# A fused decode block on one core: 768 instead of 512 columns of each partition's last wq row are loaded onto other partitions

## The chip, the core and the metric

The kernel runs on one core of a Trainium2 chip. All times are microseconds of device time. Three runs of the kernel before are shown: 137.84, 137.85 and 137.92 us, median 137.85 us. The profile is of one separate execution. A core has five engines with instruction streams of their own (TensorE, here PE, with its weight loads as PEld; VectorE, DVE; ScalarE, ACT; GpSimd, POOL; SyncE, SP), and sixteen DMA engines that move data between HBM and the on-chip memory SBUF, whose 128 partitions are the rows of every tile.

## The reference

One token for each of four sequences goes through an attention block over a window of 2048 cached keys, and then through a gated MLP. Cut to what is computed:

```python
h = x + A(layernorm(x))             # x: 4 x 1 x 1024
#   q = xn @ wq                     # wq 1024 x 4096: 32 heads of 128
#   k, v = last 2048 rows of each cache, 4 kv heads of 128
#   A = softmax(q k^T / sqrt(128)) v @ wo
h2 = h + B(layernorm(h))
#   B = (silu(hn @ w1) * (hn @ w3)) @ w2     # F = 3584
```

All inputs and the output are bf16. Weights and cache windows together make 55.6 MB that have to be read once.

## The kernel before

The kernel is a stream of large loads, all issued on SP's queue, and the arithmetic that follows it. The loads go into `ring`, one SBUF tile of 160 KiB per partition, used in a circle by hand: the `plan` list says which part of which tensor goes to which offset (`KIB = 512` elements is one KiB), and `load_next()` issues the next entry of the plan at the places in the program where its old contents have been read. The order of the stream is wq rows 0 to 3 of each partition, the side loads, wq rows 4 to 7 (the tail), the k cache (four loads), the v cache (four), wo, w1, w3, and w2 in four pieces. Semaphores made by the framework hold a load back until the readers of its place are done.

wq is laid out so that partition p holds rows 8p to 8p+7 of the 1024 x 4096 matrix (`wq_v`, `KC = 8`). For each of the eight rows the loop at line 263 issues eight matmuls of 512 columns into `q_ps`, with the matching column of the normalised x as the stationary operand (`xnT`, four columns). `JG = 4` groups of columns lie in four stripes of 32 partitions of `q_ps`.

The exception is the end of the last row. The last `CE = 512` columns of row 8p+7 are left out of the tail load (`load_tail`, L126). They come through `load_side` (L120) onto other partitions: `SETS` has triples (first row group r0, ne, ns), and a set takes ne x 4 x ns rows and puts them on ne x 4 partitions, ns pieces on each. The first set has 80 rows on 20 partitions, the second 48 rows on 12. For them the same values of x are gathered in a different order: copies into `xs` (L206), transposes into `ts_ps` (L211), copies into `xsT` (L218), and, after the fourth row's matmuls, eight small matmuls (L273) that add into the same part of `q_ps`. The row loop then skips these columns.

The side tiles of the kernel before come from the pool `ktpool`, which has four buffers that later hold transposed keys. The first seven entries of the plan are issued at the start; the eighth (v, second half) is issued at `kc == RQ - 1`, in program order before the side matmuls.

After q follow the key transposes (L319), the scores (L304), the softmax, the value matmuls (L382), wo (L411), the second layernorm, w1 and w3 (L459), silu and the product, and w2 (L492). The last w2 rows are loaded in pieces of 17, 7, 3 and 1 rows of each partition (4352, 1792, 768 and 256 KB), so that little work follows the last byte; two 512-column accumulators, `ya_ps` and `yb_ps`, take rows 17 to 27, and the residual is added into them by a matmul with the identity (L507).

Of the kernel before, what the change touches and what calls it, by code (L numbers as in the profile page):

```python
# [10 lines left out]
P = 128  # L11
# [3 lines left out]
BF16 = mybir.dt.bfloat16  # L15
# [4 lines left out]
def kernel(  # L20
# [13 lines left out]
    nc = tc.nc  # L34

    B, _, D = A_x.shape
# [5 lines left out]
    KC = D // P  # L42
# [15 lines left out]
    ktpool = ctx.enter_context(tc.tile_pool(name="ktpool", bufs=4))  # L58
    wide = ctx.enter_context(tc.tile_pool(name="wide", bufs=2))
    const = ctx.enter_context(tc.tile_pool(name="const", bufs=1))  # L60
    act = ctx.enter_context(tc.tile_pool(name="act", bufs=1))
# [3 lines left out]
    JG = 4  # L65
    QD = P // JG
    RS = QD // B
    CQ = Hq * Dh // JG
# [20 lines left out]
    ring = stream.tile([P, RING], BF16)  # L89
# [19 lines left out]
    N_Q, N_F = Hq * Dh, F  # L109


    CE = 512
    SETS = [(0, 5, 4), (80, 3, 4)]

    def load_side(r0, ne, ns):

        t = ktpool.tile([P, JG * QD * 16], BF16, tag="kT")
        rows = A_wq[r0 * KC : (r0 + ne * 4 * ns) * KC, N_Q - CE : N_Q]
        rows = rows.rearrange("(t i k) n -> k i t n", i=ne, k=KC)[KC - 1]
        nc.sync.dma_start(out=t[: ne * 4, : ns * CE], in_=rows)  # L120
        return [t[: ne * 4, k * CE : (k + 1) * CE] for k in range(ns)]

    def load_tail(at, src, n, r0, m):

        t = ring[:, at : at + m * n]
        nc.sync.dma_start(out=t[:, : m * n - CE], in_=src[:, r0 * n : (r0 + m) * n - CE])  # L126
        return [t[:, k * n : (k + 1) * n] for k in range(m)]
    KIB = 512
    plan = [
        ("wq", load_rows, (0, wq_v, N_Q, 0, 4)),  # L130
        ("side", load_side, SETS[0]),
        ("side", load_side, SETS[1]),
        ("wq", load_tail, (32 * KIB, wq_v, N_Q, 4, 4)),
        ("k", load_kv, (64 * KIB, A_k_cache, 0)),
        ("k", load_kv, (96 * KIB, A_k_cache, 2)),
# [10 lines left out]
    loaded = {}  # L146
    cursor = [0]

    def load_next(n=1):
        for _ in range(n):  # L150
            if cursor[0] < len(plan):
                kind, f, args = plan[cursor[0]]
                loaded.setdefault(kind, []).extend(f(*args))
                cursor[0] += 1
# [13 lines left out]
    for c in range(2):  # L168
        nc.sync.dma_start(
            out=x_q[c * 2 * QD : (c + 1) * 2 * QD : RS, :],  # L170
            in_=x_flat.rearrange("b (j c) -> j b c", j=JG)[2 * c : 2 * c + 2],
# [7 lines left out]
    for c in range(2):  # L179
# [8 lines left out]
        out=xn[:], in0=x_sb[:], scalar1=mv[:, 0:1], scalar2=rstd[:, 0:1],  # L188
# [9 lines left out]

    NS = sum(ns for _, _, ns in SETS)
    ts_ps = psA.tile([P, NS, B], BF16, tag="kt1")  # L200
    xs = wide.tile([B, NS, 20], BF16, tag="w4k")
    sl = []
    for r0, ne, ns in SETS:
        v = xn[:, r0 * KC : (r0 + ne * 4 * ns) * KC]
        v = v.rearrange("b (s l i k) -> b k l i s", s=4, l=ns, i=ne)
        nc.vector.tensor_copy(  # L206
            out=xs[:, len(sl) : len(sl) + ns, : ne * 4].rearrange("b l (i s) -> b l i s", s=4),
            in_=v[:, KC - 1, :, :, :],
        )
        for l in range(ns):  # L210
            nc.tensor.transpose(  # L211
                out=ts_ps[: ne * 4, len(sl), :], in_=xs[:, len(sl), : ne * 4], identity=ident[:B, :B]
            )
            sl.append(ne * 4)
    xsT = act.tile([20, NS, B], BF16)
    k0 = 0
    for _, ne, ns in SETS:
        nc.vector.tensor_copy(out=xsT[: ne * 4, k0 : k0 + ns, :], in_=ts_ps[: ne * 4, k0 : k0 + ns, :])  # L218
# [3 lines left out]
    q_ps = psA.tile([P, CQ], FP32, tag="scores")  # L222
# [9 lines left out]
        out=perm[:].rearrange("p (h dq) -> p h dq", dq=JG),  # L232
        in_=ident[:].rearrange("p (dq h) -> p h dq", dq=JG),
# [12 lines left out]
    for j in range(2, JG):  # L246
        nc.vector.tensor_tensor(
            out=same[:, 0, :], in0=same[:, 0, :], in1=ident[:, j * QD : (j + 1) * QD], op=ALU.add
# [6 lines left out]
    for kc in range(KC):  # L255
        wq_t = loaded["wq"][kc]
        for hf in range(CQ // 512):
            for g in range(JG):
                c0 = g * CQ + hf * 512
                n = min(512, N_Q - CE - c0) if kc == KC - 1 else 512  # L260
                if n <= 0:
                    continue
                nc.tensor.matmul(  # L263
                    q_ps[QD * g : QD * g + B, hf * 512 : hf * 512 + n],
                    lhsT=xnT[:, kc, :],
                    rhs=wq_t[:, c0 : c0 + n],
                    start=(kc == 0),
                    stop=(kc == KC - 1 or (kc == KC - 2 and c0 + 512 == N_Q)),
                )
        if kc == RQ - 1:  # L270
            load_next()
            for k, np_ in enumerate(sl):
                nc.tensor.matmul(  # L273
                    q_ps[QD * (JG - 1) : QD * (JG - 1) + B, CQ - CE : CQ],
                    lhsT=xsT[:np_, k, :],
                    rhs=loaded["side"][k],
                    start=False,
                    stop=False,
                )
    q_sb = act.tile([P, CQ], BF16)  # L280
    nc.vector.tensor_single_scalar(out=q_sb[:, :512], in_=q_ps[:, :512], scalar=qscale, op=ALU.mult)
    nc.scalar.mul(out=q_sb[:, 512:], in_=q_ps[:, 512:], mul=qscale)
# [1 line left out]
    for r in range(REP):  # L284
        nc.tensor.transpose(out=qt_ps[:, r, :], in_=q_sb[:, r * Dh : (r + 1) * Dh], identity=ident[:])
    nc.vector.tensor_copy(
        out=qz[:, :, : Hkv * QD].rearrange("p b (g z) -> p b g z", g=Hkv)[:, :, :, :REP],
        in_=qt_ps[:].rearrange("p r (g x) -> p x g r", g=Hkv)[:, :B, :, :],
# [24 lines left out]
    for u, (b, n) in enumerate(units):  # L313
        k_v = loaded["k"][b]
        kT = ktpool.tile([P, NJ, P], BF16, tag="kT")
        for t in range(NJ // TB):
            kt_ps = psA.tile([P, TB, P], BF16, tag=f"kt{nt % 4}")
            for jj in range(TB):
                nc.tensor.transpose(  # L319
                    out=kt_ps[:, jj, :], in_=k_v[:, n * NJ + t * TB + jj, :], identity=ident[:]  # L320
# [21 lines left out]
        out=Pm[:], in_=scores_ps[:], func=ACT.Exp, bias=nmax[:], scale=1.0, accum_out=rsum[:]  # L342
# [6 lines left out]
    for c in range(NSB):  # L349
# [4 lines left out]
        for g in range(Hkv):  # L354
            if g % 2 == 0:
                nc.vector.tensor_scalar(  # L356
                    out=z[:, :, g, :], in0=pt_ps[:], scalar1=mask[:, g : g + 1], scalar2=None, op0=ALU.mult
# [10 lines left out]
        out=Dm[:], in0=ident[:].rearrange("p (g b r) -> p b g r", g=Hkv, b=B),  # L368
# [11 lines left out]
    for b in range(B):  # L380
        for j in range(JK):
            nc.tensor.matmul(  # L382
                OT_ps[:, b, :],
                lhsT=loaded["v"][b][:, j, :],
                rhs=PTz[j // NJ][:, (j % NJ) * B + b, :, :],
                start=(j == 0),
                stop=(j == JK - 1),
# [21 lines left out]
    for i in range(IO):  # L409
        for j in range(JG):  # L410
            nc.tensor.matmul(  # L411
                y_ps[QD * j : QD * (j + 1), :],
                lhsT=o4[:, i, :, :].rearrange("p b s -> p (b s)"),
                rhs=loaded["wo"][i][:, j * CG : (j + 1) * CG],
                start=(i == 0),
                stop=(i == IO - 1),
# [27 lines left out]
        out=hn[:], in0=h1[:], scalar1=tot[:, 0:1], scalar2=rstd2[:, 0:1],  # L444
# [5 lines left out]
        out=hnT[:].rearrange("p k x -> p (k x)"), in_=hn[:].rearrange("q (c k) -> q k c", k=KC)  # L450
# [3 lines left out]
    def gate_up(kind, out_ps):  # L454
# [27 lines left out]
        out=hgT[:].rearrange("p i x -> p (i x)"),  # L482
        in_=hg[:].rearrange("q s c -> q (s c)").rearrange("q (c i) -> q i c", i=IF),
# [18 lines left out]
    for i in range(R1, IF):  # L502
        for c, t in enumerate((ya_ps, yb_ps)):
            down(i, HC, c * HC, t, start=(i == R1), stop=(i == IF - 1), skip_group_check=True)
        if i == R2 - 1:
            for c, t in enumerate((ya_ps, yb_ps)):
                nc.tensor.matmul(  # L507
                    t[:, :HC], lhsT=ident_f[:], rhs=h2[:, c * HC : (c + 1) * HC],
                    start=False, stop=False, skip_group_check=True,
# [36 lines left out]
```

## Time and profile before

| what | value |
|---|---|
| median of three runs | 137.85 us (137.84 to 137.92) |
| span of the profiled execution, first to last instruction | 136.0 us |
| what lies around the span, median less span | 1.85 us |
| PE busy, ACT busy, DVE busy | 72.3, 31.0, 43.9 us |
| DMA queue q1 (SP): share of sixteen engines' span | 95.6% |
| moved, mean rate | 55.75 MB, 410 GB/s |
| share of the DMA engines between 30 and 60 us | 1.01 |

The profile gives the span of its execution and no other time for it; the time around the span is therefore the difference to the median run. A share of the DMA engines near 1 means that all sixteen are at work. A share is counted by the transfers that start in a stretch, so that it can come out a little above 1. Next to the instructions, the trace keeps every DMA transfer with its queue, start, duration and size. A load of 128 partitions is one transfer for each partition, eight on each of sixteen engines. Each engine ends its share of a load with a transfer of 4 bytes, which counts up a semaphore.

### The profile page before, as it was taken

How to read it: one execution, taken by the hardware profiler on the slowest of the kernel's cores; microseconds unless marked ns; L12 is line 12 of the kernel's file. 1: busy time of each engine (PE TensorE's matmuls, PEld its weight loads, DVE VectorE, ACT ScalarE, POOL GpSimd, SP SyncE). 2: the span in 40 equal slices, each digit the busy share in tenths (PEclk: the TensorE clock that was granted, in tenths of full speed). 3: DMA queues.
4: the chain of work that ended last, by engine and by line, in shares of the span. 5: the costliest groups of instructions: out<-in, count | busy, mean ns of one | idle time of the engine just before them, and what ended most of it. 6: DMA issues, size and time to landing. Idle time of an engine off the chain costs nothing.

```text
span 136.0 us, 2436 instructions
## 1 busy us (share of the span) xinstructions
PE 72.3 (53%) x1096; PEld 46.1 (34%) x1096; DVE 43.9 (32%) x79; ACT 31.0 (23%) x36; POOL 1.7 (1%) x8
## 2 busy tenths in 40 slices
PE   0004920979898989810525916791097000970981
PEld 0002300268374756500014905570043000430870
DVE  5055000043344444470994001206200596026010
ACT  3000000015555555609294300000001400000000
POOL 5000000000000000000000000000000000000000
PEclk9999975557999999985555555568556855568568
DMA  5999999999999999999989999989989899999970
GB/s 155 464 463 406 412 420 414 429 424 439 424 439 424 424 443 426 410 552 453 463 347 463 463 410 405 477 354 494 439 371 494 371 472 401 399 420 407 424 298 5
DMA packets 2650, 55.75 MB, mean 410 GB/s; under 512 B 296, under 2 KB 464, under 8 KB 720
## 3 DMA queue, kind: packets, MB, share of 16 engines
q1 hardware_dynamic: 2604, 55.58, 95.6%
q8 instruction: 8, 0.13, 0.3%
q10 hardware_dynamic: 36, 0.02, 0.0%
q14 instruction: 2, 0.02, 0.0%
HBM read 55.59 MB, written 0.01 MB: 409 GB/s over the span
## 4 chain that ended last, share of the span: by engine, by line
DMA 54%; PE 25%; ACT 11%; DVE 5%; SPq 2%; issue 1%; ACTq 0%
DMA ring<-in_B_w_dram 38%; DMA ring<-in_A_wq_dram 15%; PE kt_ps L319 11%; ACT kT L325 5%; PE scores_ps L304 5%; ACT z L360 3%; PE q_ps L263 3%; DVE rmax L336 2%; ACT Pm L341 2%; PE OT_ps L382 2%; DVE pT L350 1%; SPq L120 1%; PE g_ps L459 1%; DVE z L356 1%; ACT L341 1%
## 5 line engine op out<-in xcount | busy, mean ns | idle before, releaser
L325 ACT COPY kT<-kt_ps 128x1024 bf16<-128x1024 bf16 x16 | 15.9, 1013 | 13.4 <-PE kt_ps L319 13.4
L319 PE MATMUL kt_ps<-ident,ring 128*128 128x128 bf16 x256 | 18.0, 232 | 0.0
L319 PEld LDWEIGHTS <-ring 128*128 128x128 bf16 x256 | 16.0, 105 | 4.9 <-issue 4.9
L323 DVE COPY kT<-kt_ps 128x1024 bf16<-128x1024 bf16 x16 | 11.1, 692 | 16.5 <-PE kt_ps L319 16.5
L459 PEld LDWEIGHTS <-hnT 128*32 128x32 bf16 x128 | 5.5, 143 | 21.8 <-issue 19.2
L382 PE MATMUL OT_ps<-z,ring 128*128 128x32 bf16 x256 | 7.5, 188 | 8.5 <-ACT z L360 5.0
L459 PE MATMUL u_ps<-ring,hnT 128*32 128x448 bf16 x64 | 6.0, 563 | 11.0 <-DMA ring<-in_B_w_dram 11.0
L304 PE MATMUL scores_ps<-kT,qz 128*32 128x512 bf16 x64 | 9.9, 609 | 2.9 <-ACT kT L325 2.9
L263 PE MATMUL q_ps<-ring,xnT 128*4 128x512 bf16 x63 | 6.7, 595 | 7.8 <-DMA ring<-in_A_wq_dram 7.8
L382 PEld LDWEIGHTS <-ring 128*128 128x128 bf16 x256 | 7.4, 104 | 9.2 <-issue 9.2
L459 PE MATMUL g_ps<-ring,hnT 128*32 128x448 bf16 x64 | 5.9, 558 | 4.9 <-DMA ring<-in_B_w_dram 4.9
L492 PEld LDWEIGHTS <-hgT 128*32 128x32 bf16 x156 | 4.9, 134 | 6.2 <-issue 5.7
L411 PE MATMUL y_ps<-ring,o 128*32 128x256 bf16 x128 | 5.9, 371 | 0.8 <-DVE o L398 0.8
L514 ACT CAST res<-yb_ps 128x128 bf16<-128x128 f32 x1 | 0.3, 266 | 26.1 <-PE yb_ps L492 26.1
L492 PE MATMUL y_ps<-ring,hgT 128*32 128x256 bf16 x68 | 3.8, 419 | 4.4 <-DMA ring<-in_B_w_dram 4.4
L360 ACT ACTIVATE z<-pt_ps,mask 128x512 bf16<-128x512 f32 x8 | 5.3, 687 | 3.5 <-DVE z L356 3.5
L352 PE MATMUL pt_ps<-pT,perm 128*128 128x512 bf16 x4 | 2.4, 607 | 6.8 <-DVE pT L350 6.8
L263 PEld LDWEIGHTS <-xnT 128*4 128x4 bf16 x63 | 2.0, 115 | 11.7 <-issue 11.6
L194 PE MATMUL tp_ps<-ident,xn 4*128 4x4 bf16 x8 | 0.7, 200 | 10.0 <-DVE xn L187 10.0
L356 DVE TENSOR_SCALAR z<-pt_ps,mask 128x512 bf16<-128x512 f32 x8 | 5.5, 741 | 1.2 <-ACT z L360 0.8
L473 DVE RECIPROCAL eg<-eg 128x896 f32<-128x896 f32 x1 | 5.8, 5753 | 0.0
L411 PEld LDWEIGHTS <-o 128*32 128x32 bf16 x128 | 4.4, 131 | 3.1 <-DVE o L398 1.9
(85 smaller groups left out, 50.1 us busy)
## 6 DMA issues: line engine op xcount, KB each, us to landing
ring<-in_B_w_dram SPq DMA_DIRECT2D x2, 7168.0 KB, 22.5
ring<-in_A_k_cache_dram SPq DMA_DIRECT2D x4, 2048.0 KB, 27.6
ring<-in_A_v_cache_dram SPq DMA_DIRECT2D x4, 2048.0 KB, 29.2
ring<-in_B_w_dram SPq DMA_DIRECT2D x1, 4352.0 KB
ring<-in_A_wq_dram SPq DMA_DIRECT2D x1, 4096.0 KB, 12.2
ring<-in_A_wq_dram SPq DMA_DIRECT2D x1, 3968.0 KB
ring<-in_B_w_dram SPq DMA_DIRECT2D x1, 1792.0 KB
ring<-in_B_w_dram SPq DMA_DIRECT2D x1, 768.0 KB
```

The source lines that it names most:

```text
L263: nc.tensor.matmul(q_ps[QD * g : QD * g + B, hf * 512 : hf * 512 + n], lhsT=xnT[:, kc, :], rhs=wq_t[:, c0 : c0 + n], start=(kc == 0), stop ...
L304: nc.tensor.matmul(scores_ps[QD * g : QD * (g + 1), n * 512 : (n + 1) * 512], lhsT=qz_v[:, z0 : z0 + QD], rhs=kT_v[:, g, :, :], start=(b = ...
L319: nc.tensor.transpose(out=kt_ps[:, jj, :], in_=k_v[:, n * NJ + t * TB + jj, :], identity=ident[:])
L323: nc.vector.tensor_copy(out=kT[:, t * TB : (t + 1) * TB, :], in_=kt_ps[:])
L325: nc.scalar.copy(out=kT[:, t * TB : (t + 1) * TB, :], in_=kt_ps[:])
L356: nc.vector.tensor_scalar(out=z[:, :, g, :], in0=pt_ps[:], scalar1=mask[:, g : g + 1], scalar2=None, op0=ALU.mult)
L360: nc.scalar.mul(out=z[:, :, g, :], in_=pt_ps[:], mul=mask[:, g : g + 1])
L382: nc.tensor.matmul(OT_ps[:, b, :], lhsT=loaded["v"][b][:, j, :], rhs=PTz[j // NJ][:, (j % NJ) * B + b, :, :], start=(j == 0), stop=(j == J ...
L411: nc.tensor.matmul(y_ps[QD * j : QD * (j + 1), :], lhsT=o4[:, i, :, :].rearrange("p b s -> p (b s)"), rhs=loaded["wo"][i][:, j * CG : (j + ...
L459: nc.tensor.matmul(out_ps[QD * j : QD * (j + 1), hf, :HF], lhsT=hnT[:, k, :], rhs=loaded[kind][k][:, c0 : c0 + HF], start=(k == 0), stop=( ...
L473: nc.vector.reciprocal(out=eg[:], in_=eg[:])
L492: nc.tensor.matmul(out_ps[QD * j : QD * (j + 1), :n], lhsT=hgT[:, i, :], rhs=loaded["w2"][i][:, j * CG + c0 : j * CG + c0 + n], **kw,)
```

## The change

`CE` goes from 512 to 768 and the 128 rows are dealt out differently: 96 rows on 32 partitions, 24 rows on 12, 8 rows on 4. The side tiles move from `ktpool` into `ring` at 128, 136 and 140 KiB, the place of the first half of v. So that half of v can be issued only when the side matmuls have read them, and both halves of v are now issued together, after the side matmuls in program order; the two small loads of `x_q` thereby come ahead of v on SP's queue. Since 768 columns span two PSUM banks, each side piece takes two matmuls, of 256 and 512 columns.

```diff
-    CE = 512
-    SETS = [(0, 5, 4), (80, 3, 4)]
-    def load_side(r0, ne, ns):
-        t = ktpool.tile([P, JG * QD * 16], BF16, tag="kT")
+    CE = 768
+    SETS = [(0, 8, 3), (96, 3, 2), (120, 1, 2)]
+    SIDE = [(max(CQ - CE, c), min(c + 512, CQ)) for c in range(0, CQ, 512) if c + 512 > CQ - CE]
+    def load_side(at, r0, ne, ns):
+        t = ring[: ne * 4, at : at + ns * CE]
         rows = A_wq[r0 * KC : (r0 + ne * 4 * ns) * KC, N_Q - CE : N_Q]
         rows = rows.rearrange("(t i k) n -> k i t n", i=ne, k=KC)[KC - 1]
-        nc.sync.dma_start(out=t[: ne * 4, : ns * CE], in_=rows)
-        return [t[: ne * 4, k * CE : (k + 1) * CE] for k in range(ns)]
+        nc.sync.dma_start(out=t, in_=rows)
+        return [t[:, k * CE : (k + 1) * CE] for k in range(ns)]
...
-        ("side", load_side, SETS[0]),
-        ("side", load_side, SETS[1]),
+        ("side", load_side, (128 * KIB, *SETS[0])),
+        ("side", load_side, (136 * KIB, *SETS[1])),
+        ("side", load_side, (140 * KIB, *SETS[2])),
...
-    xs = wide.tile([B, NS, 20], BF16, tag="w4k")
+    xs = wide.tile([B, NS, QD], BF16, tag="w4k")
...
-    xsT = act.tile([20, NS, B], BF16)
+    xsT = act.tile([QD, NS, B], BF16)
...
-                    stop=(kc == KC - 1 or (kc == KC - 2 and c0 + 512 == N_Q)),
+                    stop=(kc == KC - 1 or (kc == KC - 2 and c0 >= N_Q - CE)),
...
         if kc == RQ - 1:
-            load_next()
             for k, np_ in enumerate(sl):
-                nc.tensor.matmul(
-                    q_ps[QD * (JG - 1) : QD * (JG - 1) + B, CQ - CE : CQ],
-                    lhsT=xsT[:np_, k, :],
-                    rhs=loaded["side"][k],
-                    start=False,
-                    stop=False,
-                )
+                for c0, c1 in SIDE:
+                    nc.tensor.matmul(
+                        q_ps[QD * (JG - 1) : QD * (JG - 1) + B, c0:c1],
+                        lhsT=xsT[:np_, k, :],
+                        rhs=loaded["side"][k][:, c0 - (CQ - CE) : c1 - (CQ - CE)],
+                        start=False,
+                        stop=False,
+                    )
+            load_next(2)
```

## The prediction

> **What bounds the kernel now.** I read the page first, then the chain that ended last, then the work by windows of time, and last the single transfers in the trace.
>
> The page:
>
> ```profile
> span 136.0 us, 2436 instructions
> PE 72.3 (53%) x1096; PEld 46.1 (34%) x1096; DVE 43.9 (32%) x79; ACT 31.0 (23%) x36; POOL 1.7 (1%) x8
> DMA  5999999999999999999989999989989899999970
> q1 hardware_dynamic: 2604, 55.58, 95.6%
> q8 instruction: 8, 0.13, 0.3%
> ```
>
> No instruction engine is over 53% busy; the sixteen DMA engines are full from the second slice to the end. Queue q8 carries eight loads of PE's own program, which matter below. The chain of waits between 96 and 136 us (start, us, what):
>
> ```profile
> 76.27 22.49 DMA ring<-in_B_w_dram
> 98.80 1.68 PE g_ps L459 x14
> 100.48 29.74 DMA ring<-in_B_w_dram
> 130.22 0.04 issue
> 130.27 0.30 PE ya_ps L492 x3
> ...
> 131.82 0.42 PE ya_ps L507 x2
> 132.24 0.22 PE yb_ps L507 x2
> 132.46 0.17 PE ya_ps L492 x4
> ...
> 133.08 0.27 ACT res L514
> ```
>
> The end is released by w2 rows landing (130.22), then 2.8 us of PE. Windows (us, busy by engine, then granted PE clock, DMA share, GB/s):
>
> ```profile
> 30.00:60.00 30.00, 25.64 (x314) 17.27 (x311) 12.45 (x17) 15.90 (x16) 0.00 (x0) 0.96 1.01 430
> ...
> 130.60:131.10 0.50, 0.50 (x30) 0.50 (x25) 0.00 (x0) 0.00 (x0) 0.00 (x0) 0.50 0.93 369
> 131.30:131.80 0.50, 0.50 (x28) 0.40 (x17) 0.00 (x0) 0.00 (x0) 0.00 (x0) 0.75 0.65 250
> 131.80:132.20 0.40, 0.40 (x8) 0.40 (x4) 0.00 (x0) 0.00 (x0) 0.00 (x0) 1.00 0.60 230
> ```
>
> In mid stream all sixteen work (1.01); in the last microsecond only 0.60 to 0.65: some DMA engines are done early. So the end is set by the slowest DMA engine, and the even share is the quantity to follow. The trace's transfer records give it. On one engine the next transfer's record begins some 3 ns before the last one's ends, so records string into sixteen chains, and the 4-byte transfers show when each chain finishes a load. Finish times of two loads, us, sorted:
>
> ```
> wq tail: 21.39 21.50 21.53 21.64 21.64 21.66 21.70 21.73 21.76 21.85 21.95 | 22.15 22.34 | 22.97 22.99 23.30
> last w2: 130.60 130.84 131.02 131.24 | 131.88 132.00 and ten more, from 132.14 to 132.38
> ```
>
> At the tail there are eleven engines without side pieces (call them C), two with the 16 pieces of the first side load (B), and the same three with 16 of each (A): the three-way load lies on engines that also had the five-way one, so shares fill from the same end. A piece of 1024 bytes comes every 42.4 ns, 32 of them make 1.36 us; that is A's lag. By the end twelve are late. Each of the eight q8 loads (16 KB, starting at 32.0, 43.7, 54.6, 79.6, 86.1, 92.6, 105.2, 130.6) sets one chain back by 1.42 us, and the chains say that these are eight different engines, all of them in C. A program load on q14 at 60.6 cost one of B 0.85 us. So the twelve late are A, one of B (the one that also carries the four-way `x_sb` load; it ends near 132.26) and eight of C; early are the other B (131.24) and the three of C without a program load (130.60, 130.84, 131.02). The side loads before had put A level with the eight.
>
> **The change part by part.**
>
> *Tail load, 512 bytes less on 128 partitions.* Start-to-start on a full engine is 607.5 ns for 16384 bytes and 1284 for 34816, 37.6 ns per KB: 18.8 ns per transfer, eight on each engine, so every engine gains 0.150 us.
>
> *Side pieces.* 1536 bytes does not occur. Neighbours: 23.6 ns at 512 bytes, 42.4 at 1024, 79.9 at 2048; these lie on one line (18.8 per 512), which gives 61.2 ns. Bounds are 42.4 and 79.9; I take the line. The first load has 8 x 12 pieces: A, B and three of C get 12 (0.734 us). The second has 3 x 8: A (0.490). The third, 8 rows on 4 partitions, is four-way: A and one B, two each (0.122); by the same end-filling as `x_sb` I take the B with the 0.85 us.
>
> Net against before, tail included (A also has one more 4-byte transfer, 0.006):
>
> - A: 1.346 - 1.357 + 0.006 - 0.150 = -0.155
> - the B near 132.26: 0.857 - 0.678 + 0.006 - 0.150 = +0.035, so 132.30
> - the other B: 0.734 - 0.678 - 0.150 = -0.094
> - three of C: 0.734 + 0.006 - 0.150 = +0.59
> - the other eight of C: -0.150
>
> If the three of C are those without a program load they end at 131.2 to 131.6, still early. A's last goes 132.38 to 132.23, the eight's last 132.34 to 132.19, and the late B at 132.30 is then last. The stream ends 0.08 us earlier. Row prices at their bounds move A by 22 x 0.0188 = 0.41 either way: at the lower bound B still leads at -0.23 (132.03, with the eight at 132.19 last: -0.19), at the upper A ends at 132.64, +0.26.
>
> One rule of the Trainium skill speaks against the change: "DMA: Bandwidth & Descriptors", section "Latency and other measured facts", says copies whose row pitch is a large power of two run slower, at 512 KiB pitch 207 GB/s against 214. Successive pieces of one engine are 8 rows of 64 KiB apart in the new first load (320 KiB before). By it the 0.73 us would be about 0.02 longer, an estimate; no run here has such a pitch, and nothing in the sum uses it.
>
> *SP's queue.* From the timeline:
>
> ```profile
> 1.17 1.81 SPq L120 DMA_DIRECT2D t<-in_A_wq_dram  x2
> 3.03 0.44 SPq L126 DMA_DIRECT2D ring<-in_A_wq_dram  x1
> 12.94 3.14 PE L263 MATMUL q_ps<-ring,xnT 128*4 128x512 bf16 x32 [2.03 <-DMA ring<-in_A_wq_dram]
> 16.01 1.89 PE L273 MATMUL q_ps<-t,xsT 20*4 20x512 bf16 x8
> 23.66 3.58 PE L263 MATMUL q_ps<-ring,xnT 128*4 128x512 bf16 x31 [5.76 <-DMA ring<-in_A_wq_dram]
> ```
>
> Two side issues take 0.96 and 0.80 us; three take at most 2.9, so the tail is issued by 4.2 us; the engines work on the first wq half until 12.0. Cost nothing. Each load reuses a semaphore of the one eight before, so one more load shifts these waits: the third k load waits for the first wq half (12.9), `x_q` comes next and costs the same packets earlier, the first v waits for the side matmuls (about 18.5) and the second v for the tail (23.5) instead of being issued by 14.8. The four k loads keep the engines busy to 40.8, so at least 17 us cover that. wo is held by the key transposes at 42.8 either way.
>
> *PE.* L273: eight 512-column matmuls at 0.21 each; now seven of 512 and seven of 256, 1.5 + 0.8 = 2.3 instead of 1.9 us, inside the 5.8 us that PE idles before 23.66. The last row has one 512 matmul halved, -0.1. Seven transposes for eight. *DVE:* two more copies of 0.1 to 0.2 us at 10 to 11.3 us, needed at 16. All hidden; were they not, the next cover is the DMA itself, since w1 is issued at 76.27 and the first engine needs it at 79.7: 3.4 us.
>
> *Tail of the kernel.* w2's landings shift together by -0.08. PE from 130.27 runs at clock 0.50 until about 131.55, then full: starting 0.08 earlier at half speed but getting the full clock no sooner saves 0.04. The last landing, at 132.68, releases the last eight matmuls at 132.74, which move with it by the full 0.08. I take -0.08.
>
> Sum: profiled span 136.0 - 0.08 = 135.9; on the median, 137.85 - 0.08 = 137.77 (the profile's own execution has no other time; 1.85 us lie around its span). A measurement of this kernel tells about 0.2%, 0.28 us, from no change, so this is no change.
>
> **The rivals.**
>
> *The three of C do carry program loads (slower).* The eight are different engines and spare all five of A and B. If they are a block at the other end, the next three after B are the early ones. If the block begins earlier, one to three of them are hit: then 132.16 (the engine of the load at 32.0) + 0.59 = 132.75, or that of 43.7, 132.34 + 0.59 = 132.93. The end moves by +0.37 to +0.55: 138.22 to 138.40. It decides as soon as one late C engine is among the three. For it: no record names an engine. Against: none of eight loads fell on the end that fills first.
>
> *The pieces cost like 2048 bytes.* A at 132.64: +0.26, 138.11. Against: three sizes on one line.
>
> *PE's clock rises later.* The profile shows 0.50 at 130.6 and 1.00 at 131.8. Work done at the full clock from 131.55 to 133.06 would double at worst: +1.3, 139.1. Against: three runs agree within 0.08.
> The page "TensorE: Matmul & The Clock Gate", Part 1, calls the activity window of about 3.4 us free-running, so that the rise can fall elsewhere; the rises here lie a multiple of 3.41 us apart, and by the page some runs would show that cost.
>
> *The whole 0.15 or more arrives (faster).* Every engine's cut is 0.15 at most, so over 0.28 needs another gain, such as another split of the start-up lags, 0.6 us wide in C.
>
> **How the numbers follow.** Forecast 0.64 (own range 137.60 to 137.95), hit engines 0.25, dearer pieces 0.04, clock 0.03, faster 0.04. Of the first about 0.02 is faster than 0.2%; of the dearer pieces half is within it. Faster 0.06, same 0.65, slower 0.29. The range takes the cheap bound (-0.19) and the hit engines: 137.60 to 138.40.
>
> **What would show it.** In the profile after: 128 transfers of 1536 bytes about 65 ns long; tail finishes with A near 22.8 and 23.15, five engines (B and three of C) at 22.05 to 22.55, eight at 21.25 to 21.8; w1 issued within 0.3 us of 76.27; at the end twelve late engines, and the three of C in between at 131.2 to 131.6. Wrong: an engine with 12 pieces and a q8 load, ending near 132.7 to 132.9; or a DMA share clearly under 1 between 12 and 105 us, which would mean a load issued too late.

## The result, and the profile after

The changed kernel took 138.34 us (median of six runs, 138.14 to 138.62), the kernel before beside it 137.93 us (six runs, 137.84 to 138.03): a ratio of 1.0033 [1.0022, 1.0045]. It is slower, by 0.41 us. The forecast was no change (137.77 us); the price is that of the first rival, "the three of C do carry program loads".

The profile page of the changed kernel:

```profile
span 136.5 us, 2444 instructions
PE 74.5 (55%) x1101; PEld 46.3 (34%) x1101; DVE 44.1 (32%) x81; ACT 31.0 (23%) x36; POOL 1.7 (1%) x8
DMA  5999999999999999999999997999979989998960
q1 hardware_dynamic: 2611, 55.58, 95.2%
q8 instruction: 8, 0.13, 0.3%
```

The same bytes on the same sixteen engines, and again eight loads of PE's program on q8. The last slice but one is at 6 tenths where it was at 7: the last microseconds are thinner. The windows show it (us, busy by engine, then granted PE clock, DMA share, GB/s), first in mid stream, then at the end:

```profile
30.00:60.00 30.00, 25.49 (x312) 17.07 (x309) 12.56 (x17) 15.90 (x16) 0.00 (x0) 1.00 1.01 431
...
131.50:132.00 0.50, 0.50 (x33) 0.40 (x24) 0.00 (x0) 0.00 (x0) 0.00 (x0) 1.00 0.66 258
131.80:132.20 0.40, 0.40 (x18) 0.30 (x6) 0.00 (x0) 0.00 (x0) 0.00 (x0) 1.00 0.45 169
132.20:132.60 0.40, 0.40 (x8) 0.28 (x11) 0.00 (x0) 0.00 (x0) 0.00 (x0) 1.00 0.19 72
```

Mid stream is as full as before. Between 131.8 and 132.2 us the share is 0.45 where it was 0.60, and in the 0.4 us behind that it is still 0.19, or three engines of sixteen: thirteen engines are done, and three go on alone. In the kernel before that last stretch is all but empty:

```profile
132.20:132.60 0.40, 0.40 (x19) 0.28 (x21) 0.00 (x0) 0.00 (x0) 0.00 (x0) 1.00 0.05 15
```

The chain of waits between 96 and 137 us (start, us, what):

```profile
76.11 23.09 DMA ring<-in_B_w_dram
99.20 0.04 issue
99.24 1.68 PE g_ps L462 x15
100.93 29.68 DMA ring<-in_B_w_dram
130.60 0.04 issue
130.64 0.30 PE ya_ps L495 x3
...
133.02 0.06 PE yb_ps L495 x4
133.08 0.24 PE ya_ps L495 x4
133.32 0.08 PE yb_ps L495 x4
133.40 0.02 issue
133.42 0.27 ACT res L517
```

w1 is issued at 76.11, even a little earlier than the 76.27 of before, but lands 23.09 us later, not 22.49. So the loss is made between issue and landing of w1, not by a late issue. At the end PE has done all the work that it has rows for and starts the last eight matmuls only with the last landing, at 133.08.

The finish times of single engines (the 4-byte transfers at the end of each engine's share, us, sorted) say which engines are late:

```
tail     21.32 21.36 21.46 21.50 21.60 21.63 21.64 21.71 | 22.10 22.14 22.16 22.17 | 22.66 | 22.85 22.87 22.99
wo       79.54 79.58 79.68 79.92 | 80.32 80.35 80.38 80.39 | 81.14 81.21 81.24 81.26 81.26 81.28 81.29 | 81.72
w1       96.45 96.48 96.59 96.83 | 97.26 97.29 | 98.05 98.12 98.15 98.17 98.17 98.19 98.20 | 98.63 98.65 98.71
last w2  130.43 130.78 131.21 131.24 | 131.85 131.95 132.00 and six more to 132.15 | 132.58 132.60 132.66
```

In the row of the tail the four engines at 22.10 to 22.17 are the other B and the three of C, the mid group in what follows: twelve pieces, no third load. They stay together to the end of wo (80.32 to 80.39). In the row of w1 only two of them are where they should be; the other two have gone to the end of the row, 98.65 and 98.71. Two program loads began in between, at 84.55 and 90.96 us, and each set its engine back 1.42 us as the prediction had it for every such load. These two engines, with their 12 pieces of 1536 bytes and a program load, are the last to finish, at 132.60 and 132.66.

From there to the end of the span (us):

| | last 4-byte transfer | last landing | PE's end | output landed | end of span |
|---|---|---|---|---|---|
| before | 132.38 | 132.68 | 133.02 | 135.16 | 136.00 |
| after | 132.66 | 133.03 | 133.37 | 135.51 | 136.46 |
| difference | +0.28 | +0.35 | +0.35 | +0.35 | +0.46 |

So 0.35 us of the span's 0.46 arrive with the last landing; another 0.11 us appear behind the output's landing, where no work of the kernel is left. The experiments go after both.

### The profile page after: what moved, and what is told of

Same layout as the page of the kernel before. It is cut to its first block, busy times and chain, and to the rows that moved or that the text cites. A ratio compares the mean times of both kernels' runs of the same rounds, so it can differ in the third digit from the quotient of the medians.

```text
span 136.5 us, 2444 instructions
## 1 busy us (share of the span) xinstructions
PE 74.5 (55%) x1101; PEld 46.3 (34%) x1101; DVE 44.1 (32%) x81; ACT 31.0 (23%) x36; POOL 1.7 (1%) x8
## 4 chain that ended last, share of the span: by engine, by line
DMA 53%; PE 25%; ACT 11%; DVE 5%; SPq 2%; issue 1%; ACTq 0%
DMA ring<-in_B_w_dram 39%; DMA ring<-in_A_wq_dram 14%; PE kt_ps L322 11%; ACT kT L328 5%; PE scores_ps L307 5%; ACT z L363 3%; PE q_ps L265 3%; SPq L121 2%; DVE rmax L339 2%; ACT Pm L344 2%; PE OT_ps L385 1%; DVE pT L353 1%; PE g_ps L462 1%; DVE z L359 1%; PE ya_ps L495 1%
## 5 line engine op out<-in xcount | busy, mean ns | idle before, releaser
L326 DVE COPY kT<-kt_ps 128x1024 bf16<-128x1024 bf16 x16 | 11.1, 692 | 16.5 <-PE kt_ps L322 16.5
L265 PE MATMUL q_ps<-ring,xnT 128*4 128x512 bf16 (+1 forms) x63 | 7.2, 623 | 4.3 <-DMA ring<-in_A_wq_dram 4.3
L414 PE MATMUL y_ps<-ring,o 128*32 128x256 bf16 x128 | 5.3, 332 | 1.0 <-DVE o L401 0.8
L284 DVE TENSOR_SCALAR q_sb<-q_ps 128x512 bf16<-128x512 f32 x1 | 0.7, 692 | 14.4 <-PE q_ps L265 14.4
```

The costliest lines, as they stand in the source:

```text
L265: nc.tensor.matmul(q_ps[QD * g : QD * g + B, hf * 512 : hf * 512 + n], lhsT=xnT[:, kc, :], rhs=wq_t[:, c0 : c0 + n], start=(kc == 0), stop ...
L326: nc.vector.tensor_copy(out=kT[:, t * TB : (t + 1) * TB, :], in_=kt_ps[:])
L414: nc.tensor.matmul(y_ps[QD * j : QD * (j + 1), :], lhsT=o4[:, i, :, :].rearrange("p b s -> p (b s)"), rhs=loaded["wo"][i][:, j * CG : (j + ...
```

## The experiments

The edits that follow with 512 columns are made on the changed kernel, so that they keep its side tiles in `ring`, the order of the issues and both halves of v behind the side matmuls. Times in one group share the runs of the kernel before, whose median was 137.82, 137.80 and 137.83 us in the three groups.

### First group: where does it come from

**mark.** No transfer record names an engine. This kernel deals the same rows so that engine 6 and engine 7 each have a number of pieces that no other has: 28 pieces on engines 1 to 3 (counted from the end that fills first), 16 on 4 and 5, 8 on engine 6, 4 on engine 7.

```diff
-    CE = 768
-    SETS = [(0, 8, 3), (96, 3, 2), (120, 1, 2)]
+    CE = 512
+    SETS = [(0, 7, 1), (28, 6, 1), (52, 5, 2), (92, 3, 3)]
+        ("side", load_side, (144 * KIB, *SETS[3])),
-    load_next(7)
+    load_next(8)
```

> Four side loads of 512 columns dealt so that the number of 1024-byte transfers in a chain names the engine: 28 for the first three counted from the end that fills first, 16 for the next two, 8 for the sixth, 4 for the seventh, none for the eighth and the rest. Theory (the new first load puts pieces on engines that also carry program loads): of the eight q8 loads, two fall on the sixth, seventh and eighth engine, so at least one is seen on a chain with 8 or 4 pieces. Rival (program loads spare the first eight engines, and the change lost its time elsewhere): all q8 loads fall on chains without pieces. Time by the theory: a hit engine six gets 8 x 0.042 = 0.34 us, so 137.9 to 138.25 us; by the rival 137.75 to 137.95.

It took 138.08 us (one run). The chain with 4 pieces finished the tail at 21.60, that with 8 at 21.85. Both are undisturbed to the end of wo, 58.22 us later like the other undisturbed chains (79.81 and 80.07). w1 then takes an undisturbed chain 16.91 us:

```
wo       79.64 79.73 79.74 79.81 79.92 80.05 80.07 80.37 ...
+16.91   96.55 96.64 96.65 96.72 96.83 96.96 96.98 97.28
w1       96.55 96.64 96.65   -   96.83 96.96   -   97.28 ... 98.14 ... 98.40
```

The two that are missing are these two, and they appear 1.42 us later, at 98.14 and 98.40. The program loads between began at 84.30 and 90.38 us, each where a transfer of one of these two chains ended: the fifth lies on engine 6, the sixth on engine 7. Engine 6 is also the one that finishes last (132.35). So two of the three engines that the changed kernel's first side load adds to A and B are engines that carry a program load anyway. Engine 8 has no pieces in this kernel and can't be told from the others; in the changed kernel two engines of the mid group are not hit and end early (131.21 and 131.24), and by this count engine 8 is one of them. The nested counts (each engine of a shorter load has the pieces of every longer one) also agree with a sentence of the Trainium skill: "DMA: Bandwidth & Descriptors", section "Why a DMA increments its semaphore by 16 and not by 1", says that such a load on k engines takes the lowest-numbered k.

**sets512.** The new sets with the old width, so that pieces of 1024 bytes lie on the same eight engines.

```diff
-    CE = 768
+    CE = 512
```

> The changed kernel with 512 columns: the new deal of rows over 8, 3 and 4 engines, ring placement and queue order, but pieces of 1024 bytes and the tail load as long as before. Theory: 12 x 42.4 ns = 0.51 us of pieces on the two hit engines against 0.73, and 0.15 us more tail on all; their last semaphores go from 132.60 and 132.66 to 132.53 and 132.59, 0.15 to 0.2 us over the kernel before: 138.05 to 138.2 us. Rival (the time lies in the longer pieces, the second matmul of each or the halved last row): as before, 137.85 to 138.0 us.

138.20 us (138.06 to 138.34), 1.0025 [1.0015, 1.0035]. The width is not needed for the loss. Of the 0.30 us that the span grew, 0.20 come with the last landing (132.88) and the rest, as in the changed kernel, behind the output's landing.

**ring512.** The old sets and the old width; what is left of the change is the side tiles in `ring`, the order of v and `x_q`, and the issue of both halves of v behind the side matmuls.

```diff
-    CE = 768
-    SETS = [(0, 8, 3), (96, 3, 2), (120, 1, 2)]
+    CE = 512
+    SETS = [(0, 5, 4), (80, 3, 4)]
-        ("side", load_side, (140 * KIB, *SETS[2])),
-    load_next(7)
+    load_next(6)
```

> The changed kernel with the old 512 columns and the old deal (80 rows on five engines, 48 on three): only the placement in the ring, v issued after the side matmuls and the small x_q loads ahead of v are left of the change. Theory: these are covered, 137.85 to 138.0 us, and the spread of last semaphores is that of before (about 132.4). Rival (late v or the order of the queue costs the time): 138.2 to 138.4 us with a DMA share below 1 between 14 and 60 us.

137.76 us (137.68 to 138.01), 0.9997 [0.9988, 1.0006], a little under the 137.85 that was expected. Its chain of waits from 130 us on is that of before within 0.04 us:

```profile
100.50 29.75 DMA ring<-in_B_w_dram
130.25 0.04 issue
...
133.07 0.02 issue
133.09 0.27 ACT res L516
```

All that the prediction costed at nothing in SP's queue and in PE's order did cost nothing. The whole loss is in what is dealt to which engine, and in the number of loads.

**noside.** On the kernel before: no side loads at all, and the tail brings the whole last row.

```diff
-    CE = 512
-    SETS = [(0, 5, 4), (80, 3, 4)]
+    CE = 0
-        ("side", load_side, SETS[0]),
-        ("side", load_side, SETS[1]),
-    load_next(7)
+    load_next(5)
```

> The kernel before with no side loads at all: the tail load has all 32768 bytes per partition. Theory (the eight engines with a program load are the bound, and the side loads relieve them): every engine gets 8 x 37.6 ns = 0.30 us more tail, the eight end at 132.2 to 132.65 instead of 131.9 to 132.35, the first three engines end 1.06 us earlier than before: 138.1 to 138.25 us. Rival (the three engines with two side loads are the bound): 137.6 us or less.

138.12 us (138.04 to 138.48), 1.0026 [1.0016, 1.0035]. Now seven engines with a program load are last, at 132.26 to 132.54, and no other engine ends after 131.9. A, which carries none of the eight in the kernel before, is then not among the last. The last landing is 0.14 us later than before; another 0.13 us of the span lie behind the output's landing, since the number of loads is another here as well. The side loads of the kernel before thus win some 0.14 us of stream: they take bytes off the engines that carry program loads and put them on five that carry none of the eight. The change gives this up for two engines.

### Second group: the end of the program, and the dose

In the first group mark ended 0.21 us of span later than before, though its last landing was only 0.03 later. Its program issues two loads more. At the end of the program SP waits for the semaphores of the loads in a fixed order, some of them two to a wait. The queue's own waits, of the changed kernel and then of ring512 (line, what was waited for, us in total, times, longest):

```profile
SPq L544 <- DMA ring<-in_B_w_dram: 24.1, 2, 13.9
SPq L544 <- DMA out_dram<-res: 9.1, 1, 9.1
```

```profile
SPq L543 <- DMA ring<-in_B_w_dram: 30.2, 3, 24.2
SPq L543 <- DMA out_dram<-res: 1.8, 1, 1.8
```

In ring512, as before, the wait for the output is short since it comes last, behind the waits for the w2 loads. In the changed kernel the output is waited for ahead of others. Loads take eight semaphores in turn, and one load more puts the output on the next one, whose wait has two others behind it. SP's last instructions show the rest (start, us):

```
before    135.18 wait (the output's)     135.25 drain   136.00 end
ring512   135.18 wait (the output's)     135.25 drain   136.01 end
after     135.57 wait   135.63 wait      135.70 drain   136.46 end
```

The output lands at 135.16, 135.17 and 135.51; the drain follows 0.08 us later in the first two and 0.19 us later in the last.

**split512.** ring512 with the second set cut into two loads on the same three engines: one load more, and nothing else.

```diff
-    SETS = [(0, 5, 4), (80, 3, 4)]
+    SETS = [(0, 5, 4), (80, 3, 2), (104, 3, 2)]
+        ("side", load_side, (140 * KIB, *SETS[2])),
-    load_next(6)
+    load_next(7)
```

> The variant with the old deal, 512 columns and ring placement (137.76 us), its second side load cut in two of 24 rows each: the same bytes on the same engines, and one load more in the program, as in the changed kernel. Theory (the end of the program waits for eight semaphores in a fixed order, and one load more moves the output from the last of them to the first, so that seven waits of some 0.06 us or a part of them come after it): the streams end as before, output landing to the end of the span 0.95 instead of 0.84 us, 137.85 to 138.0 us. Rival (the number of loads does not matter): 137.7 to 137.85 us, 0.84 us after the landing.

137.96 us (137.81 to 138.11), 1.0010 [1.0002, 1.0019]. The last landing is at 132.68, as in before, and the span ends at 136.10: 0.951 us behind the output's landing, against 0.847 in ring512 and 0.835 before. One load more costs 0.10 us at the end of the program. The median is 0.20 us above that of ring512, which was measured in the first group; the other 0.10 us is not explained.

**eight512.** One side load of 512 columns on eight engines, sixteen pieces each, and one load fewer than before.

```diff
-    CE = 768
-    SETS = [(0, 8, 3), (96, 3, 2), (120, 1, 2)]
+    CE = 512
+    SETS = [(0, 8, 4)]
-        ("side", load_side, (136 * KIB, *SETS[1])),
-        ("side", load_side, (140 * KIB, *SETS[2])),
-    load_next(7)
+    load_next(5)
```

> 512 columns, one side load of 128 rows over eight engines: 16 pieces of 1024 bytes on each of the first eight. Theory (pieces add to the program load on the sixth and seventh engine, 42.4 ns each): 0.68 us there against 0.51 with twelve, last semaphores 132.65 to 132.85, the first three engines 0.68 us earlier than before; one load fewer, so the output is the last but one to be waited for (+0.06): 138.2 to 138.4 us, over the variant with twelve pieces (138.20). Rival (only the order and number of loads matter): below 138.0 us.

138.27 us (138.13 to 138.70), 1.0030 [1.0020, 1.0040]. The profile is of the slowest execution, 138.70 us: two of the eight engines with pieces are hit by the fifth and sixth program load, and end at 132.70 and 133.18, where 132.65 to 132.85 was expected for the usual execution. With ring512 (no piece on engines 6 and 7: 137.76), sets512 (12 pieces of 42.4 ns, 0.51 us: 138.20) and this (16 pieces, 0.68 us: 138.27) the time goes up with what these engines carry. It isn't a clean scale: sets512 and this kernel also spend 0.10 and 0.06 us more than ring512 behind the output's landing.

**after_x1.** The changed kernel with `x_sb` in one load instead of two, to bring the number of loads back.

```diff
-    for c in range(2):
-        nc.scalar.dma_start(out=x_sb[:, c * 512 : (c + 1) * 512], in_=x_flat[:, c * 512 : (c + 1) * 512])
+    nc.scalar.dma_start(out=x_sb[:], in_=x_flat)
```

> The changed kernel with x_sb loaded by one transfer of 4 x 1024 instead of two of 4 x 512, so that the program has as many loads as the kernel before. Theory: the output is waited for last again, 0.84 us from its landing to the end, 0.11 us less than the changed kernel: 138.15 to 138.3 us. Rival: as the changed kernel, 138.25 to 138.45 us.

138.33 us (138.23 to 138.37), 1.0032 [1.0019, 1.0044]: no gain over the changed kernel (138.34 in the first result, 138.18 in this group), so the expected time was missed. In the profiled execution the span did end 0.836 us behind the output's landing, like before. What took its place there is PE's clock at the end. The windows of this kernel:

```profile
131.50:132.00 0.50, 0.50 (x29) 0.50 (x23) 0.00 (x0) 0.00 (x0) 0.00 (x0) 0.50 0.71 262
131.80:132.20 0.40, 0.40 (x21) 0.27 (x13) 0.00 (x0) 0.00 (x0) 0.00 (x0) 0.70 0.45 154
```

The granted clock is still 0.50 where the changed kernel had 1.00; it rises at 132.04, not at 131.49. PE is then not ready when the last rows land, and ends 0.42 us behind the last landing instead of 0.34. That gives back 0.08 of the 0.11 us. The first work on PE also came some 5 us earlier in this kernel (5.20 us, where it was 10.12); whether that moved the rise is not shown. The rise also moves without any edit: three executions of the changed kernel have it at 131.49, 131.54 and 129.60 us. So the profile explains its own execution, and that all five runs lost the gain for this reason is not shown. In this kernel two of the four engines of the mid group (tail at 22.04 and 22.15) were again the last, at 132.51 and 132.64, hit by the eighth and the seventh program load.

**after2.** The changed kernel again, as a yardstick for this group.

> The changed kernel again, as the measure for the next three. Theory: the sixth and seventh engine again carry twelve pieces and one program load each and end last with the B that has the q14 load, last semaphores near 132.6, output landed near 135.5, 138.25 to 138.45 us. Rival (which engines take program loads differs from run to run): other engines late, and a time that jumps with it.

138.18 us (138.05 to 138.42), 1.0025 [1.0017, 1.0034], a little under the 138.25 that was expected. The last two engines ended at 132.63 and 132.78. They are two of the mid group again (tail at 22.14 and 22.29), but it was the third and the fourth program load that hit them, at 54.35 and 78.09 us: they finish wo at 81.78 and 81.92, already 1.42 us behind their place, and the fifth load begins only at 85.96. The fifth and the sixth lie on engines without side pieces in this execution.

### Third group: the count once more, and the width without the eight engines

**after_xq1.** The changed kernel with `x_q` in one load; this leaves the start alone.

```diff
-    for c in range(2):
-        nc.sync.dma_start(
-            out=x_q[c * 2 * QD : (c + 1) * 2 * QD : RS, :],
-            in_=x_flat.rearrange("b (j c) -> j b c", j=JG)[2 * c : 2 * c + 2],
-        )
+    nc.sync.dma_start(out=x_q[0:P:RS, :], in_=x_flat.rearrange("b (j c) -> j b c", j=JG))
```

> The changed kernel with x_q brought by one load of 16 partitions instead of two of 8, so that the program has as many loads as the kernel before; unlike the merged x_sb, nothing that starts PE moves. The four-way load takes 0.09 us from the first two engines and puts 0.09 on the third and fourth. Theory: the rise of PE's clock stays at 131.5, the output is waited for last again, 0.84 us from landing to end; the stream ends 0 to 0.05 later; together 0.06 to 0.12 us under the changed kernel of the same call. Rival (the earlier merge failed because the number of loads does not matter): no gain, 0.95 us after the landing.

138.14 us (137.96 to 138.34), 1.0021 [1.0013, 1.0030]; 0.20 us under after3 of the same group, where about 0.1 was expected. The changed kernel's own medians lie 0.16 us apart (138.18 to 138.34), so the size of the gain is better read from the profile. There the waits are back to the form of before, and the span ends 0.842 us behind the output's landing:

```profile
SPq L540 <- DMA ring<-in_B_w_dram: 30.1, 3, 24.2
SPq L540 <- DMA out_dram<-res: 1.8, 1, 1.8
```

Two engines of the mid group are late as in the changed kernel, hit by the third and the fourth program load (53.19 and 75.42 us) and ending at 132.69 and 132.52. One engine of A, without a program load, ends at 132.71 beside them: it finished the tail at 23.53, where A had 22.85 to 22.99 in the changed kernel. PE's clock rose at 130.62, not at 131.5 as expected; PE ended 0.34 us behind the last landing all the same. So this removes the term at the end of the program and leaves the stream about as late.

**after3.** The changed kernel once more.

> The changed kernel a third time, as the measure for the next two. Theory: 138.1 to 138.4 us, sixth and seventh engine last, output landed to end of span 0.95 us. Rival (which engines take program loads differs between runs): other engines last.

138.34 us (138.17 to 138.48), 1.0032 [1.0020, 1.0044]. Two engines of the mid group are late, at 132.41 and 132.60, hit by the sixth and the fifth program load; the span ends 0.952 us behind the output's landing.

**five768.** The new width on the old engines: nothing on 6 and 7, but pieces of 1536 bytes on A twice.

```diff
-    SETS = [(0, 8, 3), (96, 3, 2), (120, 1, 2)]
+    SETS = [(0, 5, 4), (80, 3, 4)]
-        ("side", load_side, (140 * KIB, *SETS[2])),
-    load_next(7)
+    load_next(6)
```

> 768 columns with the old deal (80 rows on five engines, 48 on three). Theory (only the sum of bytes and transfers on the slowest engine counts): sixth and seventh engine have no pieces and end 0.15 earlier than before, the first three carry 32 pieces of 61.2 ns = 1.96 us instead of 1.36 and end last, 132.38 + 0.60 - 0.15 = 132.83; as many loads as before: +0.45, 138.15 to 138.3 us. Rival (768 columns are better once the sixth and seventh engine are spared): 137.65 to 137.8 us.

138.39 us (138.11 to 138.49), 1.0033 [1.0022, 1.0044]. The last three are now A, with tail finishes of 23.36 to 23.58 and ends at 132.64, 132.65 and 132.86, where 132.83 was expected; the engines 6 and 7 are no longer late. So there is no room on A either: in the two deals of 768 columns that were run, A or the engines behind B become the slowest. Here, too, the clock rose late, at 132.50, and PE ended 0.52 us behind the last landing, where 0.34 is usual; this goes with a time above the 138.15 to 138.3 that was expected.

None of these kernels is faster than the kernel before by more than a measurement can tell; ring512 (137.76 against 137.82) is the same.

## Why the prediction was wrong

**What failed** is the step "If the three of C are those without a program load they end at 131.2 to 131.6, still early". Two engines of the mid group carried a program load, the fifth and the sixth, and ended at 132.60 and 132.66. Mark names two engines with these loads by their pieces, 6 and 7, which are two of the three of C. The prediction knew that eight of the eleven C engines are hit, and that it could not see which; it chose a block at the far end because A and B are spared, and gave the other case 0.25. Yet drawn blindly, three of eleven engines of which eight are hit are all three spared once in 165 times (3/11 x 2/10 x 1/9). Against that count the prediction had only the guess about the block. The one of the three that was not hit, and the other B, did end at 131.21 and 131.24.

**The first rival**, as it was put, is what happened: "It decides as soon as one late C engine is among the three", with the end of the stream at 132.75 to 132.93 and 138.22 to 138.40 us. Its engines ended at 132.60 and 132.66, some 0.1 to 0.3 us below, since the two finished the tail earlier (22.10 and 22.17) than the two engines that were priced would have with these pieces (22.24 and 22.43). That its total still fits has a second cause.

**A term was missing:** the end of the program. The prediction followed the shift of the semaphores by one load through the starts of loads and found it covered. It did not follow it to the last waits of SP, which nothing covers. There the one load more costs 0.11 us (0.952 behind the output's landing against 0.835; split512 adds it alone, 0.951 against 0.847, and after_xq1 takes it away, 0.842). The sum that belongs in place of -0.08 is +0.35 (last landing) + 0.11, or 0.46 us in the span.

Of the 0.35 us, 0.28 are the last engine's finish; the landing follows it by 0.37 us in the changed kernel and by 0.30 before. Over all the kernels here this step is 0.28 to 0.39 us, and what sets it is open.

**Right, point by point.**

- The piece of 1536 bytes: each of the 128 took 65.0 ns, on the line through the sizes around it. The rival of dearer pieces is out, and so is a cost of the 512 KiB pitch that the Trainium skill's rule would have added: the 96 pieces of the first load have that pitch, the other 32 have not, and all took the same.
- The tail finishes: eight engines at 21.32 to 21.71 (21.25 to 21.8 predicted), A at 22.85 to 22.99 (22.8 and 23.15), the other B and three of C at 22.10 to 22.17 (22.05 to 22.55).
- A is no longer last: all of A ended by 132.15 (132.23 predicted).
- The SP queue: w1 is issued 0.16 us earlier than before, and the DMA share is not under 1 in mid stream. ring512 shows that none of the moved issues cost anything.
- PE's clock in the changed kernel rose at 131.49 against 131.55: that rival is not the cause of this result, though the profiles of after_x1 and five768, with rises at 132.04 and 132.50, have PE end 0.08 and 0.18 us later behind the last landing.

**Wrong in size but hidden.** The late B ended at 132.58, not at 132.30. It finished the tail 0.3 us late (22.66 where 22.37 was due); what delayed it there is not shown. By itself it would have set the end only 0.08 us before the later of the two hit engines did. And the side matmuls took 4.64 us, not 2.3 (PE ran them at half rate, see the last section; in after2, the same program, they took 2.43):

```profile
16.46 4.64 PE L275 MATMUL q_ps<-ring,xsT 32*4 32x256 bf16 x14
23.46 3.58 PE L265 MATMUL q_ps<-ring,xnT 128*4 128x512 bf16 x31 [2.36 <-DMA ring<-in_A_wq_dram]
```

They delayed the first v issue to 21.13 us, where 18.5 was expected. PE still sat idle for 2.36 us behind them until the tail landed, and v was not needed by the engines before 40 us, so the covers that the prediction named did hold.

## What to carry to other kernels

Where a stream keeps all sixteen DMA engines full, the time is the load of the fullest engine, and that includes what the kernel does not issue: here eight program loads of 16 KB, each worth 1.42 us on its engine. Before bytes are moved to an engine, find out whether it has one of these, if need be by a kernel that deals every engine a different number of pieces. And a further load is paid for once more at the end (0.10 us here), if it moves the output off the last semaphore that the program waits for.

## What the runs showed of the hardware

Not every execution has the same program load on the same engine, but the number of engines of the mid group that are hit stayed the same. In every kernel whose tail finishes let the group be told apart it was two, by two loads that follow each other: the fifth and the sixth in the changed kernel and in after3 (and in mark, on engines 6 and 7, and in eight512, on two of the first eight), the third and the fourth in after2 and after_xq1, the seventh and the eighth in after_x1. This fits the same two engines each time, with the order of the loads moved by two; only mark shows by the pieces that they are engines 6 and 7. What sets the order is open.

The order of the waits at the end of a program is worth about 0.06 us for each wait that comes behind the output's: the span ends 0.84 us behind the output's landing with none (before 0.835, ring512 0.847), 0.90 with one (eight512), 0.95 with two (changed kernel, split512) and 1.02 with three (mark).

PE's rate at the start is not the same in every run. A side matmul of 512 columns was followed by the next matmul after 0.427 us in the changed kernel and in after_xq1, and after 0.215 us in before, after2 and five768. The trace's records of the granted clock agree: in before, after2 and five768 the first is a rise to 1.00 at 15.50, 15.49 and 16.45 us, while in the changed kernel and in after_xq1 there is none before 32.50 and 28.22 us. (A window that lies before the first record, like 16.5 to 21.1 us of the changed kernel, is printed with a clock of 1.00; no record stands behind it.) In after3 the first such matmul took 0.416 us and those after the rise at 16.96 us took 0.215. "TensorE: Matmul & The Clock Gate" of the Trainium skill, Part 1, says that the activity window runs freely and that the same kernel therefore does a different number of its first matmuls at half rate; the changed kernel (all seven side matmuls of 512 columns), after3 (the first) and after2 (none), which are the same program, agree. At the end of the span the rise of the clock lay between 129.1 us (sets512) and 132.5 us (five768), which is a spread of one such window of 3.4 us.
